# One subtraction of a fused convolution and expert kernel, issued on VectorE in place of GpSimd

## The chip, the cores and the metric

The kernel runs on one core of one Trainium2 chip. The metric is the device time of one execution in microseconds (us), lower is better. The time of the kernel before is the median of three runs. One further execution was recorded by the hardware profiler; all durations below are from that one, and line numbers (L1407) are those of its program.

## What is computed

The reference does two things in turn. First a causal depthwise convolution of width 7 over 8 sequences of 3584 tokens of 192 numbers, with a softmax over the 7 taps of each of 8 heads. Then a mixture of experts over all 28672 tokens: a gate gives 8 logits a token, and the (token, expert) pairs are taken in falling order of their logit, each token once and each expert 3584 tokens at most. Each token then goes through its expert:

```python
logits = x @ w_gate                      # 28672 x 8
order = np.argsort(-logits.flatten())    # greedy, each expert holds N // E = 3584 tokens
...
for e in range(E):
    mask = assigned == e
    h = np.maximum(x[mask] @ w1[e], 0.0)     # 192 -> 1024
    out[mask] = h @ w2[e]                    # 1024 -> 192
```

## The kernel before, in words

**Three kinds of work share the core.** The convolution (`build`) runs first, 16 half sequences long. The assignment of tokens to experts (`Route`) is long and serial: thresholds, rounds of counting, sorting the tokens of each expert into lists. The expert layers (`FFN`) work on 56 tiles of 512 tokens, numbered 0 to 55 in `moe_kernel`: tiles 0 to 7 are one tile of each expert, tiles 8 to 31 are three tiles of each expert (t = 1, 2, 3), tiles 32 to 55 again three of each (t = 4, 5, 6). The lists of tiles 0 to 7 and of tiles 8 to 31 are made by the first two sorts; the lists of tiles 32 to 55 only come out of the last part of the routing (`rest`, L1510), which runs beside the expert layers of the tiles before.

**A tile in the expert layers.** `FFN.run` (L1424) walks eight steps f = 0 to 7 a tile. A step issues one eighth of the first layer of tile i (`l1`: five matmuls into one PSUM bank `ph`, three of them with the tile `xa`, two with `xd`), and one eighth of the second layer of tile i-1 (`l2`: four pairs of matmuls into `y`). ScalarE makes the high part `hh` of the hidden layer and VectorE the low part `hl`; three banks `ph` are in use in turn. After each second step `yt` (ScalarE) and `yo` (VectorE) finish 128 tokens, which GpSimd scatters to the output (L1348). All operands are kept as a high and a low part of reduced precision, so that two matmuls give float32's accuracy.

**Turned tokens.** The tokens of a tile are gathered by row (`xg`, L1273, GpSimd's indirect DMA, two tiles ahead) and must be turned so that the channels lie on the partitions. Tiles 8 to 31 (`swapped`) do so in `turn` (L1388): VectorE transposes blocks (`xs<-xg`), SyncE stores them to DRAM (`scr`, L1396) and loads them back (L1398, L1399), ScalarE makes the high parts of the first 128 channels (`xa`) and of the other 64 (`xd`), and one step later the low parts are the difference of token and high part. The low part of `xa` is GpSimd's (L1407), that of `xd` VectorE's. Tiles 32 to 55 are turned by VectorE alone (`shuffle`), and there both low parts are VectorE's already.

**What sets the order.** Every engine runs its instructions in the order in which the program issues them. The routing is a chain of Python generators, and at each of many points of the expert layers `steps` calls `Steps.hook` (L95), which issues further routing steps as long as a model of the engines' time allows it. The model (`Pace`, `Meter`, L29) keeps a clock for TensorE, VectorE and ScalarE: a metered VectorE instruction of n float32 elements a partition moves VectorE's clock on by

```python
p.dve = max(p.dve, p.pe) + 0.15 + n / 960 / w        # w = 1 for float32
...
if ... or p.dve > p.pe + slack or p.act > p.pe + act: return      # slack 1.8, act 3
```

GpSimd's instructions are not metered. In `turn` the name `V` is the metered VectorE and `P` is GpSimd.

**The end of the routing.** Each of its last two sorts (`sort4`, L514) makes 16 one-hot tiles `oa` on VectorE, multiplies them on TensorE (four groups of 32 small matmuls `bg<-oa,X`), evicts the results on ScalarE (`X<-bg`), and has SyncE write them to DRAM (`otab`, L546, twice) and read them back (`X<-otab`, L563, eight loads). Then `Route.gather` (L580) multiplies what was read (`bg<-iq,ones` and sixteen `bg<-c_oh,X`), and `tokens` makes from it the lists `ib` and `jb`. `sort4` notes the model time of the last eviction plus TURN = 10 us (L565), and `gather` is held back until TensorE's model clock has passed it (L586), when it is issued by `hook`. There is a second way to issue it: at f = 0 of tile 30 the tokens of tile 32 are gathered, whose list is `jb`. `idx_of` (L1641) then issues all of the routing that is left at once, with no regard to the model's times:

```python
if bg.gens:
    bg.drain()
```

Of the kernel before, what the change touches and what calls it, by code (L numbers as in the profile page):

```python
# [6 lines left out]
F32 = mybir.dt.float32  # L7
# [4 lines left out]
OP = mybir.AluOpType  # L12
# [247 lines left out]
class Route:  # L260
# [306 lines left out]
    def turn(self):  # L567

        nc, wk = self.nc, self.wk
        A, PE = nc.scalar, nc.tensor  # L570
        OT = self.OT = wk.tile([128, 16, 128], BF, name="X2")
        self.there = None
        for q in range(2):
            ps = self.bg().bitcast(BF)
            for j in range(8):
                PE.transpose(ps[:, 128 * j:128 * j + 128], self.O[:, :, 8 * q + j], self.identb)
            A.activation(OT[:, 8 * q:8 * q + 8].rearrange("p j q -> p (j q)"), ps, AF.Copy)
            yield PEA if q else None
# [572 lines left out]
class FFN:  # L1151
# [236 lines left out]
    def turn(self, i, step):  # L1388

        V, A, S, P = self.nc.vector, self.nc.scalar, self.nc.sync, self.nc.gpsimd  # L1390
        if step < 0:
            t = self.xp.tile([128, 6, 128], F32, name="xs")
            V.transpose(t.rearrange("p k (b t) -> p b k t", b=4), self.XG.pop(i).rearrange("p b (k c) -> p b k c", c=32))
            d = self.scr[i % 2]
            for q in range(4):
                S.dma_start(d[:, :, q].rearrange("k c t -> c k t"), t[32 * q:32 * q + 32])  # L1396
            x = self.XS[i] = self.xp.tile([128, 2, 512], F32, name="xs")
            S.dma_start(x[:, 0], d[0:4].rearrange("k c q t -> (k c) (q t)"))  # L1398
            S.dma_start(x[0:64, 1], d[4:6].rearrange("k c q t -> (k c) (q t)"))  # L1399
        elif step == 3:  # L1400
            self.XT[i] = (self.xs.tile([128, 2, 512], FR, name="xa"), self.xs.tile([128, 512], FR, name="xd"))
            x, (xa, xd) = self.XS[i], self.XT[i]
            A.activation(xa[:, 0], x[:, 0], AF.Copy)
            A.activation(xd[0:64], x[0:64, 1], AF.Copy)
        elif step == 4:
            x, (xa, xd) = self.XS.pop(i), self.XT[i]
            P.tensor_tensor(xa[:, 1], x[:, 0], xa[:, 0].bitcast(F32), op=OP.subtract)  # L1407
            V.tensor_tensor(xd[64:128], x[0:64, 1], xd[0:64].bitcast(F32), op=OP.subtract)

    def prep(self, i, step):  # L1410
# [295 lines left out]
```

## Time and profile before

| what | value |
|---|---|
| time, median of 3 runs (lowest to highest) | 1246.0 us (1242.64 to 1251.04) |
| the profiled execution | 1251.99 us |
| its span, first to last instruction | 1250.2 us |
| busy: TensorE / VectorE / ScalarE / GpSimd | 97% / 78% / 44% / 43% of the span |
| mean granted TensorE clock | 0.994 |

The span is what the profile can explain; 1.8 us of the profiled execution lie outside of it. TensorE (PE) is busy 97% of the span, but its shares differ by stage: the convolution and the first lists take the first 160 us, tiles 0 to 7 with part of the routing go to about 323 us, tiles 8 to 31 to about 794 us, and the routing ends at 752 us. After it nothing but the expert layers is left. Three views are used below: busy time in stretches of the span, instructions in order of time, and the chain of work that ended last, cut to a stretch.

### The profile page before, as it was taken

To read this page: it belongs to the slowest core of one execution; us is meant where nothing else is said; L and a number is where in the kernel's file an instruction comes from. 1 tells how busy PE (TensorE), PEld (TensorE's weight loads), DVE (VectorE), ACT (ScalarE), POOL (GpSimd) and SP (SyncE) were. 2 spreads that over 40 slices of the span, in tenths; PEclk is the share of its full clock that TensorE was granted. 3 is DMA by queue.
4 is the path that set the end of the run, shared out by engine and by line. 5 is a ranking of instruction groups with operands and counts; after the bars stand their busy time and mean duration, and the time that the engine had idled before them with its cause. 6 is when DMAs were issued, how large, how long until landed. Compare 5 with 4: busy or idle time off the path is not lost.

```text
span 1250.2 us, 21752 instructions
## 1 busy us (share of the span) xinstructions
PE 1208.1 (97%) x7702; PEld 1036.5 (83%) x7702; DVE 979.4 (78%) x2131; ACT 547.4 (44%) x1220; POOL 531.7 (43%) x528
## 2 busy tenths in 40 slices
PE   4999989999999999999999989999999999999997
PEld 2445568889988989889888879999999999999996
DVE  7388669889898898989888865777777777777772
ACT  4454555656444544444543333333443333443331
POOL 3000344535455545555454434445444544444522
PEclk9999999999999999999999999999999999999999
DMA  9999889999725463444344563114133222413100
GB/s 221 339 348 310 294 299 316 280 321 302 270 82 155 128 188 113 158 149 149 123 144 135 178 164 121 36 48 154 67 126 107 95 97 96 157 56 137 49 23 28
DMA packets 125188, 205.09 MB, mean 164 GB/s; under 512 B 21440, under 2 KB 85392, under 8 KB 121360
## 3 DMA queue, kind: packets, MB, share of 16 engines
q1 hardware_dynamic: 82464, 127.22, 31.9%
q0 software_dynamic: 21504, 44.07, 11.7%
q10 hardware_dynamic: 21104, 32.34, 7.8%
q8 instruction: 62, 1.02, 0.3%
q14 instruction: 54, 0.44, 0.1%
HBM read 118.64 MB, written 84.93 MB: 163 GB/s over the span
## 4 chain that ended last, share of the span: by engine, by line
PE 85%; DVE 6%; DMA 5%; issue 1%; SPq 1%; ACT 1%; POOL 1%; ACTq 0%; POOLq 0%; DVEq 0%
PE ph L56 40%; PE y L56 38%; PE bg L56 3%; PE cv L56 3%; DMA X<-in_x_dram 2%; DVE X L56 1%; DVE aT L56 1%; DMA wgr<-in_moe_w_gate_dram 1%; DMA raw<-in_moe_w_dram 1%; DMA X<-otab 1%; PE pl L56 1%; DMA xg<-attn,ja 1%; DVE hl L56 0%; PE px L56 0%; DMA otab<-X 0%
## 5 line engine op out<-in xcount | busy, mean ns | idle before, releaser
L56 PE MATMUL y<-w,hh 128*128 128x384 f32 x1792 | 536.8, 355 | 0.0
L56 ACT ACTIVATE hh<-ph 128x512 fp32r<-128x512 f32 x448 | 267.2, 597 | 486.3 <-PE ph L56 485.2
L56 PE MATMUL y<-w,hl 128*128 128x192 f32 x1792 | 449.7, 251 | 0.0
L56 DVE SCALAR_TENSOR_TENSOR hl<-ph,hh 128x512 fp32r<-128x512 f32 x448 | 308.5, 689 | 138.6 <-ACT hh L56 134.0
L56 PE MATMUL ph<-xa,w 128*128 128x512 f32 x1344 | 395.6, 402 | 0.0
L56 PEld LDWEIGHTS y<-w,hl 128*128 128x128 f32 x1792 | 341.7, 191 | 16.4
L56 PEld LDWEIGHTS y<-w,hh 128*128 128x128 f32 x1792 | 337.1, 188 | 20.4 <-issue 2.2
L56 PEld LDWEIGHTS ph<-xa,w 128*128 128x128 f32 x1344 | 218.9, 189 | 20.2 <-issue 1.0
L1348 POOL DMA_INDIRECT out_dram<-yo,ia x128 | 138.9, 1085 | 225.9 <-DVE yo L56 188.1
L1348 POOL DMA_INDIRECT out_dram<-yo,ib x96 | 95.9, 999 | 220.1 <-DVE yo L56 212.7
L56 PE MATMUL ph<-xd,w 128*128 128x512 f32 x448 | 178.9, 399 | 1.3 <-DVE xd L56 1.3
L56 PE MATMUL ph<-xd,dl 128*128 128x512 f32 x448 | 174.6, 390 | 0.2 <-DVE dl L56 0.2
L56 DVE STREAM_TRANSPOSE xs<-xg 32x128 f32<-32x128 f32 (+2 forms) x408 | 164.8, 404 | 6.6
L1273 POOL DMA_INDIRECT xg<-attn,ja x128 | 139.3, 1088 | 47.6 <-issue 40.4
L56 PE MATMUL cv<-X,TH 118*128 118x384 f32 x256 | 101.5, 523 | 19.5 <-DVE TH L56 12.5
L1273 POOL DMA_INDIRECT xg<-attn,jb x96 | 103.4, 1078 | 29.3 <-issue 29.3
L56 ACT ACTIVATE yt<-y 128x192 f32<-128x192 f32 x224 | 73.1, 326 | 94.3 <-PE y L56 92.3
L56 DVE TENSOR_TENSOR yo<-y,yt 128x192 f32<-128x192 f32 x224 | 79.5, 355 | 41.3 <-ACT yt L56 39.2
L56 PEld LDWEIGHTS ph<-xd,w 128*128 128x128 f32 x448 | 84.3, 188 | 21.4 <-DVE xd L56 1.7
L56 PEld LDWEIGHTS ph<-xd,dl 128*128 128x128 f32 x448 | 84.5, 189 | 19.7 <-issue 0.5
L56 PEld LDWEIGHTS cv<-X,TH 118*128 118x128 f32 x256 | 45.3, 198 | 49.9 <-issue 14.1
L56 ACT ACTIVATE a<-cv 128x384 f32<-128x384 f32 x128 | 59.5, 492 | 50.8 <-PE cv L56 33.0
(238 smaller groups left out, 893.1 us busy)
## 6 DMA issues: line engine op xcount, KB each, us to landing
attn<-a ACTq DMA_DIRECT2D x16, 1344.0 KB
w<-kw SPq DMA_DIRECT2D x14, 1536.0 KB
w<-kv SPq DMA_DIRECT2D x14, 1536.0 KB
kw<-w SPq DMA_DIRECT2D x48, 256.0 KB
kv<-w SPq DMA_DIRECT2D x32, 384.0 KB
X<-in_x_dram SPq DMA_DIRECT2D x17, 672.0 KB
X<-in_x_dram ACTq DMA_DIRECT2D x15, 672.0 KB
scr<-xs SPq DMA_DIRECT2D x96, 96.0 KB
```

Of the source, the lines that this page charges most:

```text
L56: return f(*a, **k)
L1273: self.nc.gpsimd.indirect_dma_start(out=t[:, b], out_offset=None, in_=self.attn[0:rows], in_offset=bass.IndirectOffsetOnAxis(ap=idx[b], ax ...
L1348: st = self.nc.gpsimd.indirect_dma_start(out=self.out, out_offset=bass.IndirectOffsetOnAxis(ap=idx, axis=0), in_=o, in_offset=None, bounds ...
```

## The change

```diff
         elif step == 4:
             x, (xa, xd) = self.XS.pop(i), self.XT[i]
-            P.tensor_tensor(xa[:, 1], x[:, 0], xa[:, 0].bitcast(F32), op=OP.subtract)
+            V.tensor_tensor(xa[:, 1], x[:, 0], xa[:, 0].bitcast(F32), op=OP.subtract)
             V.tensor_tensor(xd[64:128], x[0:64, 1], xd[0:64].bitcast(F32), op=OP.subtract)
```

One instruction for each of tiles 8 to 31, 24 in all, of 128 partitions and 512 float32 numbers, is issued to VectorE and no longer to GpSimd. It stands ahead of the subtraction of `xd`. Since VectorE is metered, each of the 24 also moves the model's VectorE clock by 0.15 + 512/960 = 0.68 us, so that `hook` issues routing steps at other places. From tile 8 on the order of the routing's instructions among those of the expert layers differs on TensorE, VectorE, ScalarE and SyncE. Three places follow.

VectorE, tile 8, as a piece of the difference (`hl` is the low part of the hidden layer, `xa` and `xd` are the turned tokens):

```order
 L56 TENSOR_TENSOR w_3884<-raw,w_3884 128x2x192
 L56 SCALAR_TENSOR_TENSOR hl<-ph,hh 128x512
+L56 TENSOR_TENSOR xa<-xs,xa 128x512
 L56 TENSOR_TENSOR xd<-xs,xd 64x512
 L56 SCALAR_TENSOR_TENSOR hl<-ph,hh 128x512
```

The new instruction stands between two of the hidden layer's.

TensorE, the last gather of the routing. Before, it stands in tile 29, halfway (after step f = 3 and inside step f = 4; `w_8385` is the first layer's weights, `w_7888` the second's):

```order
L56 MATMUL y<-w_7888,hl 128x192
L56 MATMUL ph<-xa,w_8385 128x512 x3
L56 LDWEIGHTS ones
L56 MATMUL bg<-iq,ones 128x192
L56 LDWEIGHTS X_9383
L56 MATMUL bg<-c_oh,X_9383 128x24
...
L56 MATMUL ph<-xd,w_8385 128x512
L56 MATMUL ph<-xd,dl 128x512
```

Now, ahead of the first matmul of tile 30 (`X_9159` is what the sort multiplies, 64 times here; `X_9588` is what was read back):

```order
L56 MATMUL y<-w_7853,hl 128x192
L56 LDWEIGHTS X_9159
L56 MATMUL bg<-oa,X_9159 32x128
...
L56 LDWEIGHTS ones
L56 MATMUL bg<-iq,ones 128x192
L56 LDWEIGHTS X_9588
L56 MATMUL bg<-c_oh,X_9588 128x24
...
L56 MATMUL ph<-xa,w_8316 128x512 x3
```

The last 64 matmuls of the last sort and the gather now stand directly behind each other, with no matmul of the expert layers between them. Before, the last 64 of the sort were issued in tile 28, and the gather more than half a tile later. The gather of the sort before the last one moves from the start of tile 28 to a quarter of tile 29.

VectorE, the same place. Now (`c_bi`, `c_f`, `c_oh` are `columns`, which the gather reads; `asm` is the gather's sum, the list `jb` follows 16 instructions later):

```order
L56 SCALAR_TENSOR_TENSOR hl<-ph,hh 128x512
L56 TENSOR_SCALAR c_bi<-bg 128x8
L56 CAST c_bi<-bg 128x8
L56 TENSOR_TENSOR yo<-y,yt 128x192
L56 TENSOR_SCALAR c_bi<-c_bi 128x16
L56 TENSOR_SCALAR c_f<-c_bi 128x8 x2
L56 TENSOR_TENSOR c_oh<-iq,c_f 128x16x12
L56 TENSOR_SCALAR c_oh<-c_oh,g_293 128x16x12
L56 TENSOR_TENSOR oa<-irep_528,q 128x1024 x3
L56 TENSOR_TENSOR asm<-asm,bg 128x192
```

The last three one-hot tiles and the gather's sum stand behind each other. Before, six `hl`, three `yo` and a transpose of tiles 28 and 29 stood between them.

On SyncE the second `otab` store stands behind tile 31's `scr` stores and loads, as it did before behind tile 30's, and the eight loads `X<-otab` stand directly behind it. Before, a load of first-layer weights (`w<-kw`, 1536 KB) came next; now a load of second-layer weights (`w<-kv`, 1536 KB) does.

## The prediction

> **What bounds the kernel now.** I read the page first, then the busy time by stage, then who waits for the moved instruction, and last, in order of time, the one place where TensorE stands still in the stage that changes.
>
> ```profile
> span 1250.2 us, 21752 instructions
> PE 1208.1 (97%) x7702; PEld 1036.5 (83%) x7702; DVE 979.4 (78%) x2131; ACT 547.4 (44%) x1220; POOL 531.7 (43%) x528
> PE 85%; DVE 6%; DMA 5%; issue 1%; SPq 1%; ACT 1%; POOL 1%; ACTq 0%; POOLq 0%; DVEq 0%
> ```
>
> TensorE (PE) is busy 97% of the span and is 85% of the chain that ended last; GpSimd (POOL), which loses work, is 1% of it. A busy share is a mean, so the stage counts (columns: us, then busy us of PE, PE's weight loads, DVE, ACT, POOL, granted clock, DMA share, GB/s):
>
> ```profile
> 303.00:690.00 387.00, 386.13 (x2281) 345.70 (x2280) 340.88 (x764) 179.09 (x439) 204.20 (x184) 1.00 0.49 152
> 690.00:742.00 52.00, 51.53 (x466) 44.65 (x466) 38.78 (x77) 22.95 (x46) 21.67 (x22) 1.00 0.51 149
> 742.00:770.00 28.00, 24.68 (x140) 21.97 (x139) 13.91 (x35) 8.25 (x17) 11.63 (x11) 0.88 0.63 190
> 770.00:1213.00 443.00, 443.00 (x2521) 402.28 (x2520) 337.68 (x722) 170.02 (x339) 196.53 (x189) 1.00 0.26 89
> ```
>
> The moved instructions lie in the first three rows. There TensorE is short of being always busy by 0.9, 0.5 and 3.3 us. So the stage is TensorE's, and only the third row has something to show. The granted clock is 0.88 there, full elsewhere. The stretch itself:
>
> ```profile
> 742.42 0.26 PE L56 MATMUL bg<-iq,ones 128*128 128x192 bf16 x1
> 746.00 0.58 PE L56 MATMUL bg<-c_oh,X 128*128 128x24 bf16 x16 [3.32 <-DMA X<-otab]
> ```
>
> ```profile
> 746.00:751.00 5.00, 5.00 (x30) 4.52 (x31) 4.22 (x16) 0.60 (x1) 0.00 (x0) 0.50 0.70 272
> 751.00:752.00 1.00, 1.00 (x6) 0.86 (x5) 0.70 (x4) 0.20 (x1) 0.00 (x0) 0.76 0.00 0
> 752.00:754.00 2.00, 2.00 (x13) 1.80 (x12) 1.05 (x2) 0.72 (x2) 0.09 (x1) 1.00 0.00 0
> ```
>
> TensorE reaches the routing's last gather, and what it reads has not come back from DRAM: 3.3 us idle, the only such wait of the stage. Then it runs at half clock from 746.0 to about 751.5 (the mean of 0.76 in the row from 751 is half clock for its first half), 5.5 us at half speed, so 2.7 us are lost. This place costs 6.0 us today.
>
> **The instruction itself is worth nothing on the path.** The first three lines are GpSimd's instruction and its waits; the last is the same subtraction where tiles 32 to 55 already have it on VectorE (DVE).
>
> ```profile
> L1407 POOL TENSOR_TENSOR xa<-xs,xa x24: 1272/1287/1921, 316.1 to 766.7; 128x512 fp32r<-128x512 f32 x24
> its engine sat idle before it (us, times) until:
>   ACT xa L56: 60.5, 24
> who waited for it (us, times):
> L56 DVE TENSOR_TENSOR xa<-xs,xa x24: 680/681/684, 791.9 to 1212.6; 128x512 fp32r<-128x512 f32 x24
> ```
>
> Nothing stands under "who waited for it": it is done before tile i+1 starts. So taking 24 x 1.287 = 30.9 us from GpSimd gains 0. VectorE gets 24 x 0.681 = 16.3 us. What hides them: in the first row above VectorE is idle 387.00 - 340.88 = 46 us, and behind each subtraction stands an `hl`, for which TensorE has three banks and thus up to two further steps of 2.29 us to spare (the `ph` of two steps, below). One subtraction more puts 0.68 us in front of it. In the last stage row VectorE carries the same `xa` as well, and TensorE is busy for 443 of 443 us. If the cover failed each time, the 16.3 us would be on the path; a gain is excluded, since nobody waited. Bounds 0 to 16.3; I take 0, by the last stage row, and carry 3 us (a fifth of it) into the range.
>
> ```profile
> 754.99 0.88 PE L56 MATMUL ph<-xa,w 128*128 128x512 f32 x3
> 757.28 0.41 PE L56 MATMUL ph<-xa,w 128*128 128x512 f32 x1
> ```
>
> [...]
>
> **What the change moves is the price.** The model counts 24 x 0.68 = 16.4 us more of VectorE, so the routing is issued later: its last gather moves from the middle of tile 29 to the head of tile 30. That is more than a delay of half a tile. At the head of tile 30 `idx_of` needs the list and drains the routing, so the 10 us that the gather was held back are gone: sort, write, read and gather stand directly behind each other on TensorE, and every matmul of tile 30 is queued behind the gather. I set E for the end of the last `y` matmul before it and follow the chain.
>
> (a) VectorE's last one-hot tiles. Before, the same instructions ran here:
>
> ```profile
> 725.90 0.36 DVE L56 TENSOR_TENSOR yo<-y,yt 128x192 f32<-128x192 f32 x1 [0.17 <-ACT yt L56]
> 727.23 1.93 DVE L56 TENSOR_TENSOR oa<-irep,q 128x1024 bf16<-128x1024 bf16 x3
> 729.08 0.68 DVE L56 SCALAR_TENSOR_TENSOR hl<-ph,hh 128x512 fp32r<-128x512 f32 x1
> 729.68 0.96 DVE L56 STREAM_TRANSPOSE xs<-xg 128x768 f32<-128x768 f32 x1
> ```
>
> ```profile
> L56 ACT ACTIVATE yt<-y 128x192 f32<-128x192 f32 x224 | 73.1, 326 | 94.3 <-PE y L56 92.3
> ```
>
> `yo` waits for ScalarE's `yt` (0.33 us), which waits for E, so it starts at about E + 0.5. From its start to the first `oa` are 1.33 us, the three `oa` take 1.85 (727.23 to 729.08): E + 3.7.
>
> (b) The last sort matmuls, the eviction and the store:
>
> ```profile
> 696.63 1.19 PE L56 MATMUL bg<-oa,X 128*32 128x128 bf16 x32
> 697.39 1.09 ACT L56 ACTIVATE X<-bg 128x512 bf16<-128x512 f32 x2 [0.64 <-PE bg L56]
> 698.51 0.32 SPq L546 DMA_DIRECT2D otab<-X  x1
> 698.88 6.56 SPq L563 DMA_DIRECT2D X<-otab  x8
> ```
>
> The last `oa` feeds 8 of 32 matmuls, 0.3 us (0.6 at half clock). From the end of the 32 (697.82) to the store's issue (698.51) are 0.7 us. So the store is issued at E + 4.7 to E + 5.0, if SyncE is free: tile 31's transpose comes one step ahead of E, and SyncE was free 6.3 us after such a transpose (`xs` at 729.68 above, `otab` at 736.00 below), which is about E + 5. I take E + 4.9.
>
> (c) The round trip through DRAM, from the chain that ended last, cut to 727 to 757 us:
>
> ```profile
> 729.76 0.90 DVE xs L56
> ...
> 732.02 3.01 DMA scr<-xs
> ...
> 736.00 4.36 DMA otab<-X
> ...
> 741.73 4.08 DMA X<-otab
> 745.80 0.20 issue
> 746.00 0.58 PE bg L56 x16
> ```
>
> From the store's issue to the gather's first matmul are 10.0 us, with the same neighbours as now (a tile's `scr` ahead, a 1536 KB weight load behind). TensorE goes on at E + 14.9.
>
> (d) Of these 14.9 us TensorE uses 2 x 1.19 = 2.4 for the 64 sort matmuls, which it also had to do before. **12.5 us are new idle time, and the old 3.3 us go: +9.2 us.**
>
> (e) The half clock after it: 2.7 us before, again about that now, so 0. [...]
>
> (f) The gather of the sort before. Today it is nearly late already (the first two rows are the first and the last of the next placement's 18 matmuls):
>
> ```profile
> 698.04 0.38 PE L56 MATMUL bg<-F,U 128*128 128x512 bf16 x1 [0.22 <-ACT X L56]
> 699.31 0.22 PE L56 MATMUL bg<-U,tot 128*128 128x128 bf16 x1
> ...
> 707.87 0.26 PE L56 MATMUL bg<-iq,ones 128*128 128x192 bf16 x1
> 708.38 0.27 PE L56 MATMUL bg<-c_oh,X 128*128 128x24 bf16 x5 [0.26 <-issue]
> ```
>
> It starts 9.4 us after its store (698.51) and waits 0.26. Now three steps of 2.29 us, the placement (1.5 us) and 1.85 us of the fourth step lie between the end of its sort matmuls and it: 10.2 us, less 0.7 to the store, so 9.5. That is as close as today. 0, with up to 1.5 us against it. SyncE's eight loads then delay tile 30's `scr` by some 7 us, which ScalarE's `xa` can feel by 1 to 2 us; the spare banks hide it.
>
> Behind the drain, `hl` of tile 30 is queued behind the list's 17 small instructions on VectorE; three banks at up to 4.6 us a step (2.29 at half clock) cover that. Tile 32's tokens are needed a whole tile later.
>
> Sum: 0 + 9.2 + 0 + 0 = **+9.2 us**. The profiled execution took 1252.0 us (span 1250.2 and 1.8 outside), so it would take 1261.2; it lies 6.0 above the median, and I put the sum on the median: 1246.0 + 9.2 = **1255.2 us**, 0.7% slower. A measurement of this kernel can tell about 1% (12.5 us) from no change, so my forecast falls inside "same", on its slow side.
>
> **The rivals.**
>
> *The drain takes longer.* For: three engines and two DMA trips are in series with nothing else to run, and SyncE's queue may be later than E + 5, since the `oa` ahead of tile 31's transpose can push it back by 2.5 us; with a trip of 11.5 us it is E + 18.5, less 2.4 and 3.3: +12.8, 1258.8 us, over 1% from there. Against: the row of 10.0 us already has the same neighbours. 0.20.
>
> *VectorE becomes the bound.* Each subtraction holds up an `hl` that TensorE is waiting for: 16.3 us on top, 1271.5 us. It decides once VectorE runs more than about 4 us behind. For: 88% busy from 303 to 690. Against: 0.9 us of idle TensorE in 387. 0.05.
>
> *Half of the trip is hidden.* Of the write (4.36 us) and the read (4.08) only one is waited for, the other runs beside the sort's last part: TensorE is back at E + 4.9 + 4.3 = 9.2, less 2.4 and 3.3: +3.5 us, 1249.5. For: DMA is busy only half of the time in the stretches around. Against: the last read needs the last write, and the last write the last matmul. 0.10.
>
> *Faster.* If the gather's data come early, the 6.0 us of today's place go: 1240.0 us; and if GpSimd's slower subtraction were on the path, 24 x (1.287 - 0.681) = 14.5 us would be won: 1231.5. Against: nobody waited for it, and the order puts the gather directly behind its sort. 0.04.
>
> **How the numbers follow.** Forecast 0.61 (1252 to 1258), longer drain 0.20, half hidden 0.10, VectorE 0.05, faster 0.04. Range: below, the half hidden trip less 1.5 for the spread of the runs, 1248; above, the longer drain with a bit of (f) or VectorE's 3 us, 1262. Slower by over 1% (above 1258.5): two thirds of the longer drain, 0.13, VectorE's 0.05, and 0.09 for the forecast's own top with the spread of the runs (1242.6 to 1251.0 before): 0.27. Faster by over 1%: 0.02. Within: 0.71.
>
> **What would show it.** Right: no L1407 on GpSimd; 48 `xa<-xs` on VectorE of 0.68 us; one idle spell of TensorE of 10 to 13 us ahead of sixteen `bg<-c_oh,X`, released by `X<-otab`, near 760 us, and half clock for 3 to 7 us after it; no `bg` wait of 3.3 us in tile 29; TensorE short of 387 us by about 1 from 303 to 690. Wrong: an idle spell under 6 us there; or TensorE idle more than 4 us in total before it, waiting for `hl`; or a time below 1246.

## The result, and the profile after

| | before | after |
|---|---|---|
| median of 7 runs (lowest to highest) | 1247.56 us (1242.64 to 1251.26) | 1255.39 us (1252.41 to 1258.47) |
| ratio of the medians, 95% interval | | 1.0061 (1.0037 to 1.0085) |
| the profiled execution / its span | 1251.99 / 1250.2 us | 1255.92 / 1254.1 us |

The kernel became 0.6% slower: 7.8 us between the medians, 5 to 11 by the interval. The two profiled executions differ by only 3.9, because the one of before lies 4.4 above its median. So the profiles are compared stage by stage and not by their spans.

The head of the page of after: span, busy times, and the shares of the chain that ended last.

```profile
span 1254.1 us, 21666 instructions
PE 1207.3 (96%) x7702; PEld 1035.8 (83%) x7702; DVE 983.6 (78%) x2155; ACT 548.2 (44%) x1220; POOL 502.5 (40%) x504
PE 87%; DMA 7%; DVE 2%; ACT 1%; issue 1%; SPq 1%; POOL 1%; ACTq 0%; POOLq 0%; DVEq 0%
```

GpSimd has 24 instructions fewer and VectorE 24 more. TensorE does the same 7702 matmuls in the same busy time, and the span is longer: what was added is time in which TensorE stands still. The busy time by stage says where (us, then busy us of PE, weight loads, DVE, ACT, POOL, granted clock, DMA share, GB/s):

```profile
303.00:690.00 387.00, 387.00 (x2239) 347.83 (x2238) 335.24 (x769) 179.45 (x440) 180.93 (x165) 1.00 0.50 155
690.00:742.00 52.00, 51.09 (x462) 44.13 (x462) 45.13 (x86) 22.59 (x44) 19.14 (x18) 1.00 0.44 132
742.00:790.00 48.00, 37.62 (x266) 33.02 (x265) 25.96 (x65) 13.90 (x27) 14.91 (x15) 0.86 0.38 114
790.00:1213.00 423.00, 423.00 (x2407) 383.96 (x2406) 325.01 (x695) 162.37 (x323) 188.69 (x181) 1.00 0.27 91
```

From 303 to 690 us, where 20 of the 24 moved instructions run, TensorE is busy all the time. The third row lacks 10.4 us and has a granted clock of 0.86: the loss lies there. From the first matmul of tile 8 to that of tile 32 the trace has 471.1 us before and 476.8 after; everything behind tile 32 takes the same (456.3 and 455.8).

TensorE there, in order of time (start, duration, and in brackets idle time and what ended it):

```profile
745.88 1.19 PE L56 MATMUL bg<-oa,X 128*32 128x128 bf16 x32
747.28 0.45 PE L56 MATMUL bg<-oa,X 128*32 128x128 bf16 x8 [0.21 <-ACT X L56]
748.42 0.45 PE L56 MATMUL bg<-oa,X 128*32 128x128 bf16 x8 [0.69 <-DVE oa L56]
749.02 0.45 PE L56 MATMUL bg<-oa,X 128*32 128x128 bf16 x8 [0.15 <-DVE oa L56]
749.62 0.46 PE L56 MATMUL bg<-oa,X 128*32 128x128 bf16 x8 [0.15 <-DVE oa L56]
750.01 0.26 PE L56 MATMUL bg<-iq,ones 128*128 128x192 bf16 x1
759.44 0.58 PE L56 MATMUL bg<-c_oh,X 128*128 128x24 bf16 x16 [9.17 <-DMA X<-otab]
```

The sort's 64 matmuls, then the gather, then 9.17 us of nothing until the data are back from DRAM. The short waits ahead of it come to 1.2 us, so this place has 10.4 us of idle time, where before had 3.3. The chain that ended last shows of what the 9.17 us consist (start, duration, work):

```profile
747.77 1.81 DVE oa L56 x3
749.62 0.48 PE bg L56 x7
...
750.13 0.61 ACT X L56
...
750.75 3.62 DMA otab<-X
...
755.72 3.52 DMA X<-otab
...
759.44 0.58 PE bg L56 x16
```

One-hot tiles, matmul, eviction, write, read, gather: each piece waits for the one ahead of it, and from 750.8 to 759.2 us TensorE, VectorE, ScalarE and GpSimd are busy for 0.00 us.

### The profile page after: what moved, and what is told of

It is laid out like the page before. It is cut to its first block, busy times and chain, and to the rows that moved or that the text cites. A ratio compares the mean times of both kernels' runs of the same rounds, so it can differ in the third digit from the quotient of the medians.

```text
span 1254.1 us, 21666 instructions
## 1 busy us (share of the span) xinstructions
PE 1207.3 (96%) x7702; PEld 1035.8 (83%) x7702; DVE 983.6 (78%) x2155; ACT 548.2 (44%) x1220; POOL 502.5 (40%) x504
## 4 chain that ended last, share of the span: by engine, by line
PE 87%; DMA 7%; DVE 2%; ACT 1%; issue 1%; SPq 1%; POOL 1%; ACTq 0%; POOLq 0%; DVEq 0%
PE ph L56 41%; PE y L56 39%; PE cv L56 3%; PE bg L56 3%; DMA X<-in_x_dram 3%; DMA wgr<-in_moe_w_gate_dram 1%; DMA X<-otab 1%; PE pl L56 1%; DMA raw<-in_moe_w_dram 1%; DMA otab<-X 1%; DMA xg<-attn,ja 1%; DVE aT L56 1%; DVE X L56 0%; PE px L56 0%; ACT X L56 0%
## 5 line engine op out<-in xcount | busy, mean ns | idle before, releaser
L1348 POOL DMA_INDIRECT out_dram<-yo,ia x128 | 144.5, 1129 | 299.5 <-DVE yo L56 244.8
```

The costliest lines, as they stand in the source:

```text
L1348: st = self.nc.gpsimd.indirect_dma_start(out=self.out, out_offset=bass.IndirectOffsetOnAxis(ap=idx, axis=0), in_=o, in_offset=None, bounds ...
```

## The experiments

All are edits of the kernel before, unless it says otherwise. Each is compared with runs of before on the same chip: 1248.26 us for the first four, 1248.99 for the next four and 1248.97 for the last two.

**1. The move without its price in the model.** The subtraction is on VectorE, but the model's VectorE clock does not hear of it, so the routing is issued where it was before.

```diff
-            P.tensor_tensor(xa[:, 1], x[:, 0], ...)
+            self.nc.nc.vector.tensor_tensor(xa[:, 1], x[:, 0], ...)
```

> The subtraction is VectorE's as in the change, but the model's clock is not moved, so the routing stands where it stood before (last gather in the middle of tile 29). Theory 'order' (the time went into the forced drain at tile 30): the kernel before's time within 0.3%, that is 1244 to 1251 us beside its 1247.6; TensorE idle 3 to 4 us ahead of the last gather, as before. Rival 'instruction' (24 subtractions of 0.68 us hold up the hidden layer's low parts): as the change, about 1255 us. Rival 'relief' (GpSimd 31 us lighter helps): under 1244 us.

1247.98 us, ratio 1.0004 (0.9990 to 1.0018). TensorE at the last gather:

```profile
739.89 0.26 PE L56 MATMUL bg<-iq,ones 128*128 128x192 bf16 x1
743.34 0.56 PE L56 MATMUL bg<-c_oh,X 128*128 128x24 bf16 x16 [3.19 <-DMA X<-otab]
```

The gather is back inside tile 29, and so is the old wait of about 3 us. In the two traces TensorE, VectorE, ScalarE and GpSimd run the same instructions in the same order as before, these 24 aside. VectorE carries 24 x 0.68 us more and GpSimd 24 x 1.29 us less, and neither is to be seen in the time, which is known here to about 2 us.

**2. The price without the move.** GpSimd keeps the subtraction, and the model is told that VectorE did it.

```diff
             P.tensor_tensor(xa[:, 1], x[:, 0], ...)
+            self.nc.dve = max(self.nc.dve, self.nc.pe) + 0.15 + 512 / 960
```

> The subtraction stays on GpSimd, and only the model's VectorE clock is moved by 0.68 us for each, so that the routing stands as in the change (drained at the head of tile 30). Theory 'order': the change's time, 1252 to 1259 us, with 8 to 10 us of TensorE idle on X<-otab near 750 us. Rival 'instruction': the kernel before's time, 1244 to 1251 us.

1254.33 us, ratio 1.0056 (1.0040 to 1.0072), which lies within the interval of the change itself. TensorE in that kernel, and two rows of its chain:

```profile
749.40 0.26 PE L56 MATMUL bg<-iq,ones 128*128 128x192 bf16 x1
758.70 0.58 PE L56 MATMUL bg<-c_oh,X 128*128 128x24 bf16 x16 [9.04 <-DMA X<-otab]
```

```profile
750.13 3.48 DMA otab<-X
...
754.96 3.55 DMA X<-otab
```

The same idle spell, with no instruction moved to another engine; the order on the four engines is that of the change, the 24 aside. One and two together show that the loss comes from a number in a model of time; what the move itself adds or saves is under the 2 us that these runs can tell.

**3. The change, with more slack.** The model lets the routing run further ahead on VectorE (2.5 us in place of 1.8), so that it is issued earlier again.

```diff
-SS = (1.8, 3)
+SS = (2.5, 3)
```

> The change, with the slack of the routing's issue raised from 1.8 to 2.5 us, so that the routing is issued earlier again: sort in the first eighth of tile 29, gather five steps later (about 11.4 us), no drain. Theory 'order': no idle spell over 1 us at either gather, no half clock, 10 to 14 us less than the change: 1241 to 1246 us, below the kernel before too. Rival 'instruction': 1252 to 1258 us. Against both: VectorE running further behind lets TensorE wait for hl, several us in 303 to 690.

1242.37 us, ratio 0.9952 (0.9938 to 0.9965): faster than before. The store of the last sort and the gather:

```profile
733.84 0.58 SPq L546 DMA_DIRECT2D otab<-X  x1
...
743.83 0.55 PE L56 MATMUL bg<-c_oh,X 128*128 128x24 bf16 x16
```

The gather comes 10.0 us after the store and nothing stands in brackets: it waits for nothing, and the old 3.3 us are gone too. (Before, TensorE reached the gather 6.7 us after the store, at 742.68, and so waited for the rest of the ten.) This and the next run are not evidence for the subtraction's new engine: they remove the wait that both kernels have.

**4. Before, with the gather held back longer.** The subtraction stays on GpSimd.

```diff
-TURN = 10.0
+TURN = 13.0
```

> The kernel before with the gather held back by 13 us instead of 10 (six steps, 13.7 us, behind its sort). It tests what the kernel before loses at its own last gather. Theory 'order': the 3.3 us wait and the 2.7 us of half clock go, 6 us less than before: 1240 to 1243 us. Rival (that wait is an accident of the one profiled execution): within 2 us of before.

1243.59 us, ratio 0.9966 (0.9953 to 0.9979).

```profile
732.25 0.35 SPq L546 DMA_DIRECT2D otab<-X  x1
...
745.43 0.55 PE L56 MATMUL bg<-c_oh,X 128*128 128x24 bf16 x16
```

13.2 us lie between store and gather, filled with matmuls of the expert layers. By the medians the wait before the change was worth 4.7 us; the prediction had put that place at 6.0. By the two profiles tiles 8 to 31 are 6.3 us shorter (464.8 against 471.1), but the profiled execution of before is one that lies above its median. The hold applies to all three sorts whose gather reads from DRAM, so the order changes from tile 4 on.

**5. The subtraction twice** (the first edit, issued two times).

> As e1_unpriced (subtraction on VectorE, model clock not moved, routing in the old order), and the subtraction is done twice in tiles 8 to 31, so VectorE has 24 x 0.68 = 16.3 us more still. By the trace of e1_unpriced the first hl behind the subtraction has 1.8 to 6.8 us to spare before TensorE would wait for its bank, so theory 'order' expects no cost: within 2 us of e1_unpriced, 1246 to 1250 us. Rival 'instruction': 6 us or more above it.

1251.44 us, ratio 1.0016 (1.0003 to 1.0028), 1.4 us above what was expected. In the profiled execution TensorE is short of 387 us by 2.9 from 303 to 690, in waits under 1 us for VectorE's counts of the routing. So the cover seems to have an end, and a near one; the cost is hardly clear of the noise.

**6. The subtraction six times** (`for _ in range(6):` ahead of the first edit).

> The same with the subtraction done six times, 3.4 us more a tile than e1_unpriced. It measures how much cover there is. Adding up over the 24 tiles what 3.4 us exceed the spare time of the first hl behind it in e1_unpriced's trace gives 9 us of waiting for TensorE, more where the delay carries on to the next: theory 'order' with three banks as cover expects 8 to 16 us above before, 1256 to 1264 us, with many short TensorE waits for hl from 315 to 700 us. If the cover is larger than thought: under 1252 us; if each is on the path: 24 x 3.4 = 82 us, 1330 us.

1318.31 us, ratio 1.0558 (1.0534 to 1.0583). This missed: what I expected from the three banks was 1256 to 1264. The stage, and what TensorE waited for most from 303 to 800 us (us in total, times, longest):

```profile
303.00:690.00 387.00, 347.45 (x1878) 308.22 (x1877) 347.96 (x759) 155.45 (x388) 151.63 (x141) 0.95 0.42 129
```

```profile
PE bg L56 <- DVE r_cc L56: 17.2, 5, 5.5
PE ph L56 <- DVE hl L56: 13.8, 11, 2.7
PE bg L56 <- DVE r_v L56: 6.1, 2, 3.5
PE bg L56 <- DVE r_c L56: 3.8, 1, 3.8
```

VectorE itself is busy for only 348 of 387 us: the engines wait for each other in turn. VectorE works during 45 of the 49 us in which TensorE stands still in tiles 8 to 31, and from 303 to 690 us it waits 26 us for ScalarE's `hh` and `yt`, which are made from TensorE's results. The largest waits are not for `hl`, which has three banks, but for the routing's counts (`r_cc`, `r_v`, `r_c`): a matmul reads them, and in the longest of its waits, 5.5 us, TensorE ran nothing else. The clock falls after some of these waits; the place of the longest, in stretches of 6, 2, 6 and 3 us:

```profile
405.00:411.00 6.00, 2.83 (x16) 2.28 (x15) 5.82 (x9) 0.93 (x3) 1.77 (x1) 1.00 0.44 148
411.00:413.00 2.00, 0.00 (x0) 0.00 (x0) 1.92 (x5) 0.00 (x0) 0.00 (x0) 0.79 0.00 0
413.00:419.00 6.00, 5.67 (x18) 4.99 (x18) 5.11 (x12) 1.07 (x3) 4.26 (x4) 0.50 0.36 98
419.00:422.00 3.00, 3.00 (x20) 2.78 (x19) 2.01 (x5) 1.06 (x2) 2.39 (x3) 1.00 0.67 213
```

After the idle time TensorE works six us at half clock. Over the whole stage its idle time is 49 us, against 4 in the first experiment, and the stretches at half clock make up 51 us (the granted clock is 0.95 from 303 to 690 us, 0.98 from there to 780 and 0.96 to 860), of which half is lost at most, 26. The two account for the 69 us.

**7. The first edit with the longer hold** (`TURN = 13.0`).

> The subtraction on VectorE with the model's clock not moved, and the gather held back by 13 us. Theory 'order': as the kernel before with 13 us, 1243.6 us, within 2 us, since neither engine of the subtraction matters. Rival 'relief' (a GpSimd lighter by 31 us shows once the wait is gone): under 1241 us.

1242.02 us, ratio 0.9939 (0.9922 to 0.9957). This is the lowest median of the study: 7 us below the kernel before, and about 13 below the change. Its interval just overlaps with that of the fourth kernel, which has the same hold with the subtraction on GpSimd and otherwise the same order on the four engines, so what VectorE adds to it is not shown.

**8. The first edit, the longer hold and the larger slack together.**

> The subtraction on VectorE with the model's clock not moved, slack 2.5 us and the gather held back by 13 us: the routing stands earliest, the last gather six steps behind its sort at 29.4 tiles. Theory 'order': nothing is left to win at the gathers, so 1241 to 1244 us as e3_slack_2_5 and e4_hold_13. If an earlier routing wins by itself: under 1240 us.

1245.20 us, ratio 0.9981 (0.9964 to 0.9997), above the expected range. Tiles 8 to 31 are the shortest of all kernels (463.5 us), but tiles 0 to 7 now contain a new wait, in TensorE's order of time:

```profile
257.45 0.90 PE L56 MATMUL px<-ident,xg 128*64 128x128 f32 x4 [3.02 <-DVE xa L56]
```

These tiles take 165.0 us, where the other kernels have 160.7 to 163.7. It takes both settings: at this place the third kernel, with the same slack, waits 0.6 us twice, and the fourth and seventh, with the same hold, up to 0.4. The longer hold also moves the gather of an earlier sort, so VectorE begins on its lists at 250.4 us and no longer at 247.5, and `xa` is queued behind them. Numbers that hold for the whole program repair one place and spoil another.

**9. Four times**, to see how the cover ends.

> Before with the subtraction on VectorE at no price in the model, and issued four times. Once and twice it cost 0 and about 2 us, six times 70 us. Theory A (VectorE's idle time is one purse, some 46 us from 303 to 690 us, out of which 11.6 us go per copy): four copies just use it up, 1250 to 1262 us. Theory B (the cover ends after two copies, each further copy lies on the path with 24 x 0.68 = 16.3 us): 1249 + 2 x 16.3 = 1278 to 1286 us. In either, TensorE's waits for the hidden layer's low part and for the routing's counts should show first where the routing's counting runs, before 690 us.

1276.44 us, ratio 1.0225 (1.0183 to 1.0268).

```profile
303.00:690.00 387.00, 366.97 (x2082) 326.92 (x2081) 354.83 (x796) 168.88 (x418) 167.71 (x154) 0.99 0.45 140
```

```profile
PE bg L56 <- DVE r_cc L56: 10.3, 5, 2.7
...
PE ph L56 <- DVE hl L56: 2.8, 4, 1.3
```

The idea that VectorE's idle time is one purse (theory A, up to 1262 us) falls: 32 us of VectorE are still unused and TensorE already lacks 20. The other one comes nearer, but is not met either: one, two, four and six copies cost 0, 2, 27 and 69 us, so the first ones are nearly free, and further ones cost 13 to 21 us each. That is more at the end than their own 16.3: from four to six copies TensorE's idle time in tiles 8 to 31 grows by 24 us, 12 a copy, and its time at half clock by 38 us (mean granted clock 0.990 and 0.978 of the span), of which half at most is lost. The waits stand where the theory put them, at the counts first.

**10. Before, with the hold at 14 us.** The gather moves to the head of tile 30, where the change has it too, and the last 64 matmuls of the sort into the first third of tile 29.

> Before, GpSimd keeps the subtraction, the only edit is the gather's hold, 14 us in place of 10. The last gather then stands at the head of tile 30, as with the change, but the last sort stays in tile 29 and 64 matmuls of the sort are not directly ahead of it. Theory (the price is the missing distance between sort and gather): no wait of more than 1 us ahead of the sixteen small matmuls, about 1241 to 1246 us. Rival (the price is the place, the head of tile 30 with what the drain issues there): an idle spell of 5 us or more and 1250 us or above.

1245.56 us, ratio 0.9975 (0.9955 to 0.9995): the time is as the theory had it, but the wait is larger than its limit of 1 us. TensorE, then SyncE's queue:

```profile
747.70 0.26 PE L56 MATMUL bg<-iq,ones 128*128 128x192 bf16 x1
749.92 0.58 PE L56 MATMUL bg<-c_oh,X 128*128 128x24 bf16 x16 [1.97 <-DMA scr<-xs]
```

```profile
733.11 0.58 SPq L1231 DMA_DIRECT2D w<-kw  x1
733.79 0.45 SPq L1232 DMA_DIRECT2D dl<-kd  x1
734.28 0.58 SPq L546 DMA_DIRECT2D otab<-X  x1
734.91 12.26 SPq L563 DMA_DIRECT2D X<-otab  x8
```

The store now stands behind two weight loads (1536 and 256 KB) and not ahead of them. The chain gives its write 10.7 us, and from store to gather it is 15.6 us. The bracket names a `scr` store, which the gather does not read. In the trace's record of single transfers the last data of `X<-otab` move at 748.47, 1.5 us ahead of the gather (1.7 to 2.0 us where the bracket names `X<-otab`), so the wait is probably for these; that is inferred. The place at the head of tile 30 is thus not the price in itself: with the sort 15.6 us ahead, TensorE waits 2 us there and not 9. What counted here is the distance, and against which transfers the trip runs (the write took 10.7 us here and 3.6 after the change).

## Why the prediction was right, step by step

- **The instruction itself, 0: right, for a narrower reason than I gave.** The first experiment measured 1.0004 for it alone. But my cover (VectorE's 46 us of idle time, and `hl` with two steps to spare) is not what limits it. Experiments 5, 6 and 9 show that two copies are nearly free, four are not, and that the routing's counts are waited for before `hl` is.
- **The end of the one-hot tiles and the store, E + 3.7 and E + 4.9: right.** The last `y` matmul ends at 745.96. The `oa` end at 749.58 (E + 3.6) and the store is issued at 750.75 (E + 4.8).
- **The round trip, 10.0 us: too long.** It took 8.7 (750.75 to 759.44), and 8.6 in the second experiment. The write took 3.6 in place of 4.4 us, the read 3.5 in place of 4.1. I had taken the neighbours to be the same. The tile's two `xs` loads were issued directly ahead of the store before; after the change they are issued 1.8 us ahead of it. In the record of single transfers all 192 packets of these loads were still to come when the store was issued before, and 44 after; the write's own first packet follows its issue by 1.6 us before and 0.8 after. That accounts for the write. Why the read is shorter stays open.
- **The new idle time, 12.5 us, less the old 3.3: mis-sized.** 10.4 us are new: 1.3 less by the shorter trip, and 0.7 less because the sort's 64 matmuls, the last in pieces of 8 behind each `oa`, and the gather's first one take 3.1 us in place of 2.4. The old wait did go. The sign named for this, one idle spell of 10 to 13 us, was missed: the spell itself is 9.2 us, and 10.4 only with the short waits ahead of it.
- **The half clock, 0: nearly.** The clock at the place after the change, in stretches of 1 and 2 us:

```profile
759.00:760.00 1.00, 0.56 (x17) 0.59 (x17) 0.00 (x0) 0.00 (x0) 0.00 (x0) 0.50 0.95 406
760.00:762.00 2.00, 2.00 (x6) 1.61 (x6) 1.91 (x9) 0.00 (x0) 0.00 (x0) 0.50 0.94 399
762.00:763.00 1.00, 1.00 (x4) 0.90 (x4) 0.93 (x6) 0.60 (x1) 0.00 (x0) 0.50 0.04 12
763.00:764.00 1.00, 1.00 (x6) 1.00 (x6) 0.93 (x5) 0.00 (x0) 0.00 (x0) 0.58 0.00 0
764.00:766.00 2.00, 2.00 (x13) 1.79 (x12) 0.37 (x1) 0.57 (x1) 1.65 (x2) 1.00 0.12 28
```

  From 759.4 to about 763.8 TensorE works at half clock (a pair of `y` matmuls follows the one ahead by 0.53 us there, by 0.29 at full clock), so 2.2 us are lost where it was 2.7. The 0 was an estimate of mine from the one wait of before. The sign, half clock for 3 to 7 us, holds the 4.4; its limits were an estimate too, and no run shows them as limits. The nine-us wait cost no more of it than the one of three.
- **The gather of the sort before, 0 and up to 1.5 against: 0.7.** It waits 0.69 us at 728.8, where it waited 0.26.
- **The waits behind the drain, hidden: right.** Behind the gather TensorE has no further wait over 0.1 us until tile 32.

The sum was +9.2 us. TensorE's idle time in tiles 8 to 31 grew from 4.7 to 11.3 us and the half clock cost 0.5 less: +6.1, and the stage grew by 5.8 in the two profiles. The medians differ by 7.8. The profile of before has 6.8 us of half clock at its wait, 5.5 of them work; the first experiment, with the same order, has 3.4, and against its stage (469.6 us) that of the change is 7.2 us longer. That the predicted 1255.2 lies so close to 1255.39 is in part two errors that cancel: the sum was 1.4 above the measured difference, and the three runs on which I put it have a median 1.6 below that of seven.

Of the rivals, the longer drain is refuted (the trip was shorter), and so is the half-hidden one: in the chain, the read starts when the write has ended (the write at 754.37, the first load's issue at 754.39). VectorE as the bound shows clearly only with four copies. "Faster" needed the gather's data to come early; the third experiment shows that state, and it took another edit to reach it.

The theory that stands is this: the price is set by where a model puts the last sort and its gather, and by how much other work of TensorE stands between them. Its rival, that the subtraction costs VectorE or frees GpSimd, makes nothing of this loss: the price alone gives it, the move alone does not.

## What to carry to other kernels

Where a model of time decides the order, an instruction that moves to another engine has two prices, its own and that of the order; issue it once without telling the model, and once only tell the model, before you judge the engine. A wait on a DRAM round trip was cured here by distance between the store and its reader on the waiting engine (10.0 us in the third experiment, 13.2 in the fourth); look also at what has been queued ahead of the store. Spare room on an engine was no purse here that could be spent to its end (with four copies 32 us of VectorE stayed unused while TensorE lacked 20): ask which small results that engine makes that somebody waits for with no buffer between.

## What the runs showed of the hardware that was not expected

- The same wait was followed by two sizes of half clock. Before, 3.3 us of idle time were followed by 5.5 us of work at half clock, until 751.5; in the first experiment 3.2 us were followed by 3.4 us of it, from about 743.6 to 747.1. Rows of before, of the first experiment and of the change:

```profile
743.00:744.00 1.00, 0.00 (x0) 0.00 (x0) 0.02 (x1) 0.00 (x0) 0.85 (x2) 1.00 1.95 215
744.00:745.00 1.00, 0.00 (x0) 0.00 (x0) 0.00 (x0) 0.00 (x0) 0.40 (x1) 0.82 0.43 98
745.00:746.00 1.00, 0.00 (x1) 0.03 (x2) 0.00 (x0) 0.00 (x0) 0.00 (x0) 0.50 0.86 344
```

```profile
743.00:744.00 1.00, 0.66 (x17) 0.69 (x18) 0.06 (x1) 0.00 (x0) 0.00 (x0) 0.82 0.93 393
744.00:746.00 2.00, 2.00 (x7) 1.81 (x8) 1.97 (x9) 0.60 (x1) 0.00 (x0) 0.50 1.01 430
746.00:747.00 1.00, 1.00 (x5) 1.00 (x5) 0.97 (x3) 0.00 (x0) 0.00 (x0) 0.50 0.98 303
747.00:748.00 1.00, 1.00 (x6) 0.83 (x6) 0.93 (x3) 0.00 (x0) 0.00 (x0) 0.97 0.01 0
```

```profile
744.00:750.00 6.00, 4.79 (x77) 3.38 (x76) 5.10 (x14) 2.62 (x5) 0.00 (x0) 1.00 0.39 97
750.00:752.00 2.00, 0.27 (x5) 0.10 (x1) 0.00 (x0) 0.60 (x1) 0.00 (x0) 0.55 0.63 236
752.00:754.00 2.00, 0.00 (x0) 0.00 (x0) 0.00 (x0) 0.00 (x0) 0.00 (x0) 0.50 0.94 269
```

  Before, the clock fell 2.0 us into the wait, at about 744.65; in the first experiment 0.3 us behind the wait's end; after the change at about 750.2, just as the wait of 9.2 us began. Why it fell at these times is not shown.
- Half clock also followed on a shorter stop. With the hold at 14 us, TensorE stood still for 1.97 us and then ran at half clock for 3.4 us. In the kernel with four copies, four us with TensorE busy for 1.44 of them (400 to 404) were followed by a clock of 0.50 (404 to 406), and four with 1.60 (358 to 362) by a clock of 1.00 (362 to 364).
- A 512 KB write to DRAM took 3.6 us after the change, where nothing was issued in the 1.8 us ahead of it (3.5 us in the second experiment), 4.4 us before, directly behind a tile's two loads, and 10.7 us with the hold at 14 us, directly behind weight loads of 1792 KB on the same queue.
